# A gated attention unit and an MLP in one kernel: second batch's z moved up, blank matmuls at the start, four squares on GpSimd

## The chip, the cores and the metric

The kernel runs on one NeuronCore of a Trainium2 chip. Its engines work side by side, each through its own queue in order, and wait for each other by semaphores: TensorE (PE) does matmuls, VectorE (DVE) and ScalarE (ACT) do elementwise work, GpSimd (POOL) does elementwise work on SBUF and issues some of the DMAs, SyncE (SP) issues the others. The metric is the device time of one execution in microseconds (us); less is better.

## The reference

```python
def _attn_ref(u, v, z):                       # u, v: 8 x 3008 x 256, z: 8 x 3008 x 64
    scores = (1.0 / S) * np.matmul(z, z.transpose(0, 2, 1))
    attn = np.maximum(scores, 0.0) ** 2
    return u * np.matmul(attn, v)

def _moe_ref(x, w_in, w_out):                 # x: 24064 x 256, w_in: 256 x 2048, w_out: 2048 x 256
    h = x @ w_in
    g = h * (1.0 / (1.0 + np.exp(-1.702 * h)))
    return g @ w_out
```

The second function works on the rows that the first one makes: attention with squared relus in place of a softmax, gated by u, and then a two-layer MLP with a quick GELU.

## The kernel before

**Units.** A batch has 3008 rows. They are cut into six supercolumns of 512 rows (the last has 448), and one batch and supercolumn is a unit; there are 48. For a unit the kernel makes the scores of all 3008 rows of z against its 512 columns, in 12 pairs of two 128-row tiles. `scores` (L250) issues the two matmuls of a pair into one PSUM tile of 128x1024 (there are two such tiles, shared with the hidden layer), `relu` (L290) reads it into a 128x1024 f16 tile on ACT or DVE, and `squared` (L276) squares that tile in place, on ACT or DVE. `values` (L393) multiplies the squares with v, tile by tile ("products" below, matmuls of 64x256, always two at a time on the two halves of the array). The sums leave PSUM in two parts on ACT or DVE (`leave`, L380), POOL adds the parts (`add`, L376) and multiplies by u (`gate`, L418).

**Symmetry.** Scores are symmetric, so within a batch later units reuse squares of earlier ones: SP turns a square tile with a DMA transpose into a tile T (`turn`, L231, the issue at L242), and units from the fourth on (NDIR = 3) read these. The turned rows of units are also transposed (`turn_x`, L318) and swapped in halves (`swap_x`, L336) to feed the MLP.

**Where squares lie.** Most squares lie in a ring of 14 tiles. For units 0 and 1, pairs 6 to 11 lie in buffers that are not needed yet (`home`, L200): unit 0's in the second v buffer V16[1], unit 1's in the second turned z, ZT[1], and in z16. These must be read out before the second batch's z and v are loaded there.

**The second batch's z.** `load_z` (L105) issues three DMAs from POOL into z16, `turn_z` (L116) copies z beside itself on POOL (L118) and lets SP transpose it into ZT (L119). The first scores of unit 6 read ZT[1]. v comes in four quarters (`load_v`, L98). All of these are hooked to places in the order of work by `at` (L593): `at(n, j, ...)` runs when unit n's products reach its tile j. Each starts with `hold` (L221), a small POOL copy that reads the newest square, so that POOL's queue waits until that square is there. W1 is loaded by eight POOL DMAs at (0, 13) (L112), W2 by one at (1, 12) (L602).

**The MLP.** `hidden` (L486) makes two 128-column tiles of the hidden layer for 512 rows, ACT takes the sigmoid (L500), DVE multiplies (L504), and `outs` (L520) multiplies with w_out (L531). It runs LAG = 3 units behind the attention.

**The order of work.** The order is not written out by hand. The Python code that builds the program keeps a clock for each engine (`now`) and a price for each operation (`cost`, L131), and hands out work in the order that these give: `work` (L556) is the fixed order of products and outputs on PE; between them, `filler` (L666) puts the next score pair or hidden tile, whichever is due first; `advance` (L152) gives relus, squares and sums to the engine that would end them first, and sends DMAs on SP in order of their due time. A DMA issued by POOL, a hold and the copy in turn_z have no price in that plan. What the plan fixes is only the order on each engine; on the chip, semaphores set the times.

**The start.** z of batch 0 is loaded by SP, cast, and turned on PE through PSUM (L612 to L653), while eight blank matmuls (L625) run ahead of it.

```python
home[(0, 6 + k)] = lend(V16[1].rearrange("p n d -> p (n d)"), k)
...
at(0, 12, lambda: load_u(0))
at(0, 13, load_w1, lambda: load_u(1))
at(1, 12, lambda: pool.dma_start(W2, moe_w_out.rearrange("(fo p) c -> p fo c", p=P)))
```

Of the kernel before, what the change touches and what calls it, by code (L numbers as in the profile page):

```python
# [8 lines left out]
F32 = mybir.dt.float32  # L9
F16 = mybir.dt.float16  # L10
P = 128
# [3 lines left out]
def kernel(  # L15
# [11 lines left out]
    ALU = mybir.AluOpType  # L27

    B, S, D = u.shape
# [15 lines left out]
    LAG = 3  # L45
    RING = (LAG + 1) * TB
    H = P // 2
# [50 lines left out]
    def load_v(b, q):  # L98
        rows(b, v, q * VN, (q + 1) * VN, V16[b % 2][:, q * VN:(q + 1) * VN, :], pool)
# [5 lines left out]
    def load_z(b):  # L105
        rows(b, z, 0, NJ, z16[:, :, 0, :], pool)
# [9 lines left out]
    def turn_z(b):  # L116
        turned.add(b)
        pool.tensor_copy(z16[:, :, 1, :], z16[:, :, 0, :])  # L118
        sp.dma_start_transpose(ZT[b % 2], z16.rearrange("p n a d -> p (n a d)"))  # L119
# [9 lines left out]
    T_LAT, T_SEM, T_DMA = 0.25, 0.1, 3.5  # L129
    now = {"pe": 6.0, "act": 6.0, "dve": 7.0, "pool": 6.0, "sp": 6.0}  # L130
    cost = {  # L131
        ("act", "relu"): 1.03, ("dve", "relu"): 1.23, ("act", "sq"): 1.03, ("dve", "sq"): 0.7,
        ("act", "part"): 0.6, ("dve", "part"): 0.7, ("pool", "add"): 1.1, ("act", "sig"): 1.03, ("dve", "gt"): 1.23, ("pool", "gate"): 1.2,
        ("sp", "turn"): 1.45, ("sp", "turn_x"): 2.6, ("sp", "store"): 0.6, ("sp", "swap"): 1.2,
    }
    BOTH = ("act", "dve")
# [7 lines left out]
    def push(ready, kind, engines, fn):  # L144
        nonlocal pushed
        pushed += 1
        ops.append((ready, pushed, kind, engines, fn))
# [28 lines left out]
    def pe_at(rows_, dur):  # L176
        if mode[0] != rows_:
            now["pe"] += T_SW
            mode[0] = rows_
        now["pe"] += dur  # L180
        return now["pe"] + T_LAT
# [68 lines left out]
    def scores(k):  # L250

        nonlocal nxt
        for i in range(k):
            n, t = pairs[nxt]
            nxt += 1
            b, isup = divmod(n, NIS)
            Z = ZT[b % 2]
            assert b in turned
            p_ = take_ps()
            sc = psA.tile([P, 2, ISUP], F32, name="sc", tag="A")  # L260
            for g in range(2):
                h0 = g * DQK
                pe.matmul(  # L263
                    sc[:, g, :], Z[h0:h0 + DQK, 2 * t + g, :],
                    Z[h0:h0 + DQK, isup * NIB:(isup + 1) * NIB, :],
                    start=True, stop=True,
                )
            if (n, t) in home:
                a = home[(n, t)]
            else:  # L270
                a = pap.tile([P, 2, ISUP], F16, name="ap_", tag="ap_")
                ring.append((n, t))
            A[(n, t)] = a
            a_left[(n, t)] = 2 + turns(n, t)

            def squared(e, at, n=n, t=t, a=a, isup=isup):  # L276
                if e == "act":
                    act.activation(a, a, AF.Square, scale=1.0)
                else:
                    dve.tensor_tensor(a, a, a, ALU.mult)  # L280
                if isup == NIS - 1 and t == NP - 1:
                    pool.memset(a[:, 1, ISUP - SREM:], 0.0)
                    at += 0.5
                A_at[(n, t)] = at
                latest[0] = a
                if turns(n, t):
                    key = (n - isup + t // 2, isup)
                    send(at, "turn", NDIR if n == 1 and (n, t) in home else key[0], lambda at: turn(n, t, at), lambda: key in T or len(colors) > 0)

            def relu(e, at, p_=p_, sc=sc, a=a, squared=squared):  # L290
                if e == "act":
                    act.activation(a, sc, AF.Relu, scale=CSC)
                else:
                    dve.tensor_scalar(a, sc, 0.0, CSC, ALU.max, ALU.mult)
                set_ps(p_, at)
                push(at, "sq", BOTH, squared)

            push(pe_at(H, T_SC), "relu", BOTH, relu)

# [64 lines left out]
    def half(x, g):  # L364
        return x[g * H:(g + 1) * H]
# [227 lines left out]
    def at(n, j, *fns):  # L593
        def go():
            hold()
            for f in fns:
                f()
        side[(n, j)] = go
# [4 lines left out]
    for b in range(1, B):  # L603
        n0 = (b - 1) * NIS
        late = b == 1
        at(n0 + 1 + 2 * late, 13, lambda b=b: load_z(b))
        at(n0 + 2 + 2 * late, 13, lambda b=b: turn_z(b))
        for q in range(VQ):
            at(n0 + 3 + late + q // 2, (EDGE, 12)[q % 2], lambda b=b, q=q: load_v(b, q))


    NZ = NJ // 4  # L612
# [18 lines left out]
    def turn_q(q):  # L631
        ztps.append(psB.tile([P, NZ, P], F16, name="ztp", tag=f"B{q % 2}{q // 2}"))
        for jj in range(NZ):
            pe.transpose(ztps[q][:, jj, :], z16[:, q * NZ + jj, :, :].rearrange("p a d -> p (a d)"), ident)  # L634
# [13 lines left out]
    cast_z(3)  # L648
    keep_q(2)
    turn_q(3)  # L650
    now["pe"] = 8.0
    advance(7.0)
    keep_q(3)  # L653
# [12 lines left out]
    def filler():  # L666

        p_ = ps_free[ps_next % 2]
        if p_ is None or p_ > now["pe"]:
            return None  # L670
        can = []
        if nxt < len(pairs) and pairs[nxt][0] // NIS in turned and min(now["act"], now["dve"]) < now["pe"] + 0.8:
            old = len(ring) - NA
            if pairs[nxt] in home or old < 0 or not a_left[ring[old]]:
                can.append((urgent(("a",) + pairs[nxt], 3.0), "a"))
        if hnext < len(hids) and hnext - outs_done < NG and now["act"] < now["pe"] + 1.5 and now["dve"] < now["pe"] + 2.0:
            m = hids[hnext][0]
            xt = xt_at[m * TB // 64:(m + 1) * TB // 64]
            if None not in xt and max(xt) <= now["pe"]:
                can.append((urgent(("h",) + hids[hnext], 5.0), "h"))  # L680
        return min(can, default=None)

    wi = 0
    while wi < len(work):
        advance(now["pe"])
        w = work[wi]
        r = ready_of(w)
        late = r is None or r > now["pe"]
        f = filler()
        if f:  # L690
            if f[1] == "a":
                scores(1)
            else:
                hidden(*hids[hnext])
                hnext += 1
            continue
        if late:
            step = min([t for t in [r, ps_free[ps_next % 2]] + [o[0] for o in ops + sends] + [now[e] for e in ("act", "dve", "pool", "sp")] if t is not None and t > now["pe"]], default=now["pe"] + 0.1)
            now["pe"] = step
            assert now["pe"] < 2000.0  # L700
            continue
        if w[0] == "o":
            key = (w[1], w[2][0])
            if key in side and w[3] == 0:
                side.pop(key)()
            values(*w[1:])
        elif w[0] == "r":
            halves(w[1])
        elif w[0] == "s":
            shorts(w[1])  # L710
        else:
            outs(*w[1:])
        wi += 1
# [34 lines left out]
```

## Time and profile before

| | us |
|---|---|
| median of three runs | 1251.13 (1250.79, 1251.19, 1251.13) |
| the profiled execution | 1251.23 |
| its span, first to last instruction | 1249.3 |
| PE busy | 1228.6 (98%) |
| weight loads (PEld) busy | 1011.8 (81%) |
| DVE busy | 937.6 (75%) |
| ACT busy | 819.1 (66%) |
| POOL busy | 472.5 (38%) |

The profile is of one execution. A group's row names the line of the kernel, the engine, the operation, what it writes and reads, with shapes, how often, the busy time and the mean duration. "sc" is a score tile, "ap", "V", "ZT" and "z" as targets of L292, L294, L278 and L280 are relus and squares (the last three in borrowed buffers), "O" the sums of a unit, "hg" the hidden layer, "yps" the output. The granted clock is 1.00 when PE runs at full speed. A matmul's shown duration includes its latency; the pace of PE is better read from the chain of waits, where back-to-back products take 0.87 us for 16 and a score pair 0.22.

### The profile page before, as it was taken

How to read it: one execution, taken by the hardware profiler on the slowest of the kernel's cores; microseconds unless marked ns; L12 is line 12 of the kernel's file. 1: busy time of each engine (PE TensorE's matmuls, PEld its weight loads, DVE VectorE, ACT ScalarE, POOL GpSimd, SP SyncE). 2: the span in 40 equal slices, each digit the busy share in tenths (PEclk: the TensorE clock that was granted, in tenths of full speed). 3: DMA queues.
4: the chain of work that ended last, by engine and by line, in shares of the span. 5: the costliest groups of instructions: out<-in, count | busy, mean ns of one | idle time of the engine just before them, and what ended most of it. 6: DMA issues, size and time to landing. Idle time of an engine off the chain costs nothing.

```text
span 1249.3 us, 41891 instructions
## 1 busy us (share of the span) xinstructions
PE 1228.6 (98%) x18584; PEld 1011.8 (81%) x18584; DVE 937.6 (75%) x906; ACT 819.1 (66%) x933; POOL 472.5 (38%) x447
## 2 busy tenths in 40 slices
PE   8998999999999999999999999999999999999998
PEld 5876789988998877888778887788877888778886
DVE  7975877777888778876788768877688776877556
ACT  7855676666767657766577656676566765766444
POOL 5443334332433324343343424343343434332331
PEclk8999999999999999999999999999999999999999
DMA  9997887766986939889398684969759877574211
GB/s 151 172 166 153 145 138 131 133 132 123 133 149 135 154 91 143 142 138 165 77 142 155 128 147 90 139 125 166 131 105 141 161 127 119 112 137 110 67 45 60
DMA packets 442135, 161.74 MB, mean 129 GB/s; under 512 B 351841, under 2 KB 441953, under 8 KB 441953
## 3 DMA queue, kind: packets, MB, share of 16 engines
q1 hardware_dynamic: 390528, 141.62, 59.0%
q0 software_dynamic: 51424, 17.44, 13.8%
q8 instruction: 145, 2.38, 0.8%
q14 instruction: 38, 0.30, 0.1%
HBM read 60.29 MB, written 24.64 MB: 68 GB/s over the span
## 4 chain that ended last, share of the span: by engine, by line
PE 93%; DVE 5%; issue 1%; DMA 0%; ACT 0%; DVEq 0%; ACTq 0%
PE O L403 36%; PE hg L493 25%; PE yps L531 24%; PE sc L263 6%; PE O L478 1%; DVE GT L504 1%; PE O L465 1%; DMA ZT<-z 0%; PE warm L625 0%; DVE sums L384 0%; PE ztp L634 0%; DVE ap__8041 L280 0%; DVE ap__2880 L280 0%; DVE ap__713 L280 0%; DVE ap__18581 L280 0%
## 5 line engine op out<-in xcount | busy, mean ns | idle before, releaser
L504 DVE TENSOR_TENSOR GT<-hg,tsg 128x1024 f16<-128x1024 f32 x376 | 456.7, 1220 | 211.1 <-ACT tsg L500 209.9
L500 ACT ACTIVATE tsg<-hg 128x1024 f16<-128x1024 f32 x376 | 380.9, 1023 | 274.8 <-PE hg L493 248.2
L377 POOL TENSOR_TENSOR sums<-sums 128x512 f32<-128x512 f32 x188 | 249.0, 1325 | 666.4 <-ACT sums L382 349.4
L493 PE MATMUL hg<-XT,W 64*128 64x512 f16 x1504 | 387.9, 376 | 3.0 <-DVE GT L504 1.9
L531 PE MATMUL yps<-W,GT 64*128 64x256 f16 x6016 | 374.2, 270 | 1.3 <-DVE GT L504 0.9
L493 PE MATMUL hg<-XS,W 64*128 64x512 f16 x1504 | 370.3, 376 | 0.0
L531 PEld LDWEIGHTS <-GT 64*128 64x128 f16 x6016 | 324.1, 94 | 47.5 <-DVE GT L504 1.4
L493 PEld LDWEIGHTS <-W 64*128 64x128 f16 x3008 | 175.9, 94 | 87.5 <-issue 6.1
L403 PE MATMUL O<-V,T 64*128 64x256 f16 x3392 | 217.4, 269 | 0.1
L403 PEld LDWEIGHTS <-T 64*128 64x128 f16 x3392 | 185.9, 94 | 28.1 <-issue 0.3
L419 POOL TENSOR_TENSOR X<-sums,RU 128x512 f16<-128x512 f32 (+2 forms) x104 | 140.6, 1353 | 7.8
L263 PE MATMUL sc<-ZT 64*128 64x512 f16 x688 | 126.6, 380 | 10.7 <-DMA ZT<-z 4.5
L382 ACT ACTIVATE sums<-O 128x512 f32<-128x512 f32 x114 | 65.2, 596 | 52.8 <-PE O L403 47.1
L384 DVE TENSOR_SCALAR sums<-O 128x512 f32<-128x512 f32 x78 | 52.9, 687 | 33.9 <-PE O L403 30.1
L382 ACT ACTIVATE sums<-yps 128x512 f32<-128x512 f32 x111 | 63.8, 592 | 17.1 <-PE yps L531 15.9
L384 DVE TENSOR_SCALAR sums<-yps 128x512 f32<-128x512 f32 x73 | 50.0, 685 | 14.1 <-issue 9.9
L263 PEld LDWEIGHTS <-ZT 64*128 64x128 f16 x688 | 40.1, 95 | 17.8 <-issue 7.6
L87 POOL DMA_DIRECT2D V<-in_v_dram x32 | 28.0, 878 | 0.0
L87 POOL DMA_DIRECT2D z<-in_z_dram x7 | 10.9, 1564 | 0.4 <-PE hg L493 0.4
L478 PE MATMUL O<-V,T 128*64 128x256 f16 x160 | 10.3, 275 | 0.0
L118 POOL COPY z<-z 128x1536 f16<-128x1536 f16 x7 | 10.2, 1452 | 0.0
L478 PEld LDWEIGHTS <-T 128*64 128x64 f16 x160 | 8.1, 110 | 1.9 <-issue 1.9
(1536 smaller groups left out, 1522.2 us busy)
## 6 DMA issues: line engine op xcount, KB each, us to landing
out_dram<-sums SPq DMA_DIRECT2D x92, 256.0 KB, 4.0
RU<-in_u_dram SPq DMA_DIRECT2D x40, 512.0 KB, 4.5
V<-in_v_dram POOLq DMA_DIRECT2D x24, 384.0 KB, 7.2
XS<-XT SPq DMA_DIRECT2D x60, 128.0 KB, 4.0
RU<-in_u_dram SPq DMA_DIRECT2D x8, 384.0 KB, 3.7
z<-in_z_dram POOLq DMA_DIRECT2D x7, 368.0 KB, 9.4
V<-in_v_dram POOLq DMA_DIRECT2D x8, 320.0 KB, 9.1
XT<-X SPq DMA_TRANSPOSE x144, 2.5
```

The lines of the kernel that those rows point to most:

```text
L87: eng.dma_start(dst[:, :full - lo, :], dram[b, lo * P:full * P].rearrange("(n p) d -> p n d", p=P),)
L263: pe.matmul(sc[:, g, :], Z[h0:h0 + DQK, 2 * t + g, :], Z[h0:h0 + DQK, isup * NIB:(isup + 1) * NIB, :], start=True, stop=True,)
L377: pool.tensor_tensor(s_[:, 0, :, :], s_[:, 0, :, :], s_[:, 1, :, :], ALU.add)
L382: act.activation(s_[:, g, :, :], ps[g], AF.Copy, scale=scale)
L384: dve.tensor_scalar(s_[:, g, :, :], ps[g], scale, None, ALU.mult)
L403: pe.matmul(O[g][:, i2, :], half(sq, g), half(V[:, j, :], g), start=(j == 0 and i2 == 0), stop=(ends and j == js[-1] and (i2 == 1 or short)),)
L419: pool.tensor_tensor(X[:p, :, ib:ib + k, :].rearrange("p c n d -> p n c d"), both[:p, ib - 2 * h:ib - 2 * h + k, :].rearrange("p n (c d) - ...
L478: pe.matmul(O[c0:c0 + SREM, 1, :], squares_of(n, j, NIB - 1)[:, :SREM], V[:, j, :], start=False, stop=False, tile_position=(0, c0),)
L493: pe.matmul(hg[:, e, :], half(W1[:, fg // 2, c, fg % 2 * P:(fg % 2 + 1) * P], e), half(x[:, c // 2, p0:p0 + TB], e), start=(c == 0), stop= ...
L500: act.activation(tsg, hg, AF.Sigmoid, scale=1.702 / FSC)
L504: dve.tensor_tensor(GT, hg, tsg, ALU.mult)
L531: pe.matmul(Y[g][:, i2, :], half(GT[:, e, s * P:(s + 1) * P], g), half(W2[:, ff, :], g), start=(fg == 0 and e == 0 and i2 == 0), stop=(end ...
```

## The change

There are four edits.

1. In the plan, GpSimd gets a price for squares, and pairs 7 and 10 (t % 3 == 1) of units 0 and 1 are squared by GpSimd alone.
2. For the second batch, `load_z` is hooked to (3, 8) in place of (3, 13), and `turn_z` to (4, 6) in place of (4, 13). The first quarter of v, which was at (4, 6), goes to (4, 7).
3. Where the plan has PE wait before its first products, it now issues a blank matmul (64 rows, 256 columns, into a PSUM tile of its own); there come to be 16 of them.
4. Hidden tiles of the first 512 rows are not taken as filler before unit 3.

Nothing else is edited, but the plan is made anew: the order of PE, ACT, DVE, POOL and SP differs up to PE's matmul 3421 of 18584 and is the same from there on.

```diff
-        ("act", "relu"): 1.03, ("dve", "relu"): 1.23, ("act", "sq"): 1.03, ("dve", "sq"): 0.7,
+        ("act", "relu"): 1.03, ("dve", "relu"): 1.23, ("act", "sq"): 1.03, ("dve", "sq"): 0.7, ("pool", "sq"): 2.8,
...
-                    dve.tensor_tensor(a, a, a, ALU.mult)
+                    (dve if e == "dve" else pool).tensor_tensor(a, a, a, ALU.mult)
...
-                push(at, "sq", BOTH, squared)
+                push(at, "sq", ("pool",) if (n, t) in home and t % 3 == 1 else BOTH, squared)
...
-        at(n0 + 1 + 2 * late, 13, lambda b=b: load_z(b))
-        at(n0 + 2 + 2 * late, 13, lambda b=b: turn_z(b))
+        at(n0 + 1 + 2 * late, 8 if late else 13, lambda b=b: load_z(b))
+        at(n0 + 2 + 2 * late, EDGE if late else 13, lambda b=b: turn_z(b))
         for q in range(VQ):
-            at(n0 + 3 + late + q // 2, (EDGE, 12)[q % 2], lambda b=b, q=q: load_v(b, q))
+            at(n0 + 3 + late + q // 2, (EDGE + late, 12)[q % 2], lambda b=b, q=q: load_v(b, q))
...
+    idle = psB.tile([P, D], F32, name="idle", tag="B00")
...
-            if None not in xt and max(xt) <= now["pe"]:
+            if None not in xt and max(xt) <= now["pe"] and (m or work[wi][1] >= LAG or work[wi][0] == "y"):
...
             step = min([t for t in [r, ps_free[ps_next % 2]] + [o[0] for o in ops + sends] + [now[e] for e in ("act", "dve", "pool", "sp")] if t is not None and t > now["pe"]], default=now["pe"] + 0.1)
+            if wi == 0 and step - now["pe"] > 0.08:
+
+                pe.matmul(idle, half(blank[:, 0, :P], 0), half(blank[:, 0, :D], 0), start=True, stop=True)
+                pe_at(H, T_MM)
+                continue
```

In POOL's new queue, unit 0's pair 7 is squared first; then come the two holds of (0, 12) and (0, 13) and the eight issues of W1; then the square of unit 0's pair 10; then unit 0's sums and gates; then the square of unit 1's pair 7, the hold and issue of W2, and the square of unit 1's pair 10.

## The prediction

> **What bounds the kernel now.** I read the page's slices first, then the list of waits, then a table by stretch, then the timeline around the two places where TensorE (PE) stops. The slices:
>
> ```profile
> PE   8998999999999999999999999999999999999998
> ...
> PEclk8999999999999999999999999999999999999999
> ```
>
> PE is full nearly everywhere, at full clock; only the first slice (31 us) and the third fall short. In instruction order the two kernels become the same, on every engine, from PE matmul 3421 of 18584 on, which runs at 247.5 us. So what the change is worth arises before that. The list of waits (waiter, releaser: us in total, times, longest) and the table by stretch (PE, weight loads, DVE, ACT, POOL busy; granted clock; DMA):
>
> ```profile
> PE sc L263 <- DMA ZT<-z: 4.5, 1, 4.5
> PE hg L493 <- DVE GT L504: 1.9, 2, 1.5
> PE sc L263 <- DVE ap__809 L294: 1.7, 1, 1.7
> ...
> PE sc L263 <- DVE ap__473 L294: 1.4, 1, 1.4
> ```
>
> ```profile
> 10.60:17.30 6.70, 5.75 (x50) 4.22 (x51) 4.26 (x5) 4.67 (x5) 0.00 (x0) 0.50 1.11 150
> 17.50:24.00 6.50, 6.50 (x112) 5.87 (x110) 5.80 (x7) 5.27 (x6) 2.47 (x6) 1.00 0.68 166
> 24.00:64.00 40.00, 35.37 (x572) 31.02 (x567) 38.35 (x38) 34.21 (x39) 22.37 (x19) 1.00 1.28 170
> 102.00:106.10 4.10, 0.00 (x0) 0.00 (x0) 0.00 (x0) 0.77 (x1) 2.09 (x2) 1.00 1.07 195
> 106.20:109.50 3.30, 3.29 (x30) 2.17 (x32) 1.82 (x2) 1.54 (x2) 0.57 (x2) 0.50 0.00 0
> ```
>
> Three stages: 10.6 to 17.4 at half clock, PE the bound; 24 to 64 with DVE busy 38.35 of 40 us, so DVE is the bound and PE waits for relus; and 102 to 109.5, where PE waits for the second batch's turned z and then runs at half clock.
>
> **Blank matmuls.** From 11.55 to the first matmul on unit 0's pair 10 (24.0 us) the chain of waits has full-clock pieces of 0.87 us for 16 product matmuls and 0.22 for a score pair, half-clock pieces of 1.71 and 0.43. That stretch is 140 products and 9 score pairs in the new order: 140 x 0.0547 + 9 x 0.216 = 9.6 us at full clock from 12.0 us, where the products start in both. PE gets there at 21.6, not 24.0: 2.4 to 2.6 us sooner. The 16 blanks lie in waits for relus (0.9, 0.3 and 1.1 us) and cost at most 16 x 0.109 = 1.7 us if that cover is gone. Lower bound of the gain: 0, since the clock fell at 10.5 after a stretch in which PE was 57% busy, and blanks may not keep it. I take all of it.
>
> **Four squares by GpSimd (POOL).** Pairs 7 and 10 of units 0 and 1. POOL's queue is in order, and in the new order unit 0's pair 10 stands behind two holds and W1's eight DMA issues:
>
> ```profile
> 20.40 0.17 POOL L223 COPY scrap<-V 1x2 f16<-1x2 f16 x1 [10.82 <-DVE V L280]
> 21.41 0.17 POOL L223 COPY scrap<-V 1x2 f16<-1x2 f16 x1 [0.83 <-ACT V L278]
> 21.88 4.93 POOL L112 DMA_DIRECT2D W<-in_moe_w_in_dram  x8 [0.30 <-issue]
> ```
>
> The planner gives these issues no time; they took 4.93 us. Both holds now wait for pair 9's square, on DVE, which by the sooner PE ends at about 19.5 (before, 22.4). Then 0.1 + 2 x 0.17 + 0.3 + 4.93: the square starts at 25.2. No row shows such a square. Low end: the copy L118, 1.452 us for 1536 elements, so 0.97 for 1024. High end: L377, 1.72 us for 512 when DVE interferes, so 3.44. L377 is nearest (two inputs, an elementwise operation), at its mean of 1.325: 2.65. It ends at 27.9, and PE, in order, stands at pair 10's products from 21.6: a new wait of 6.3 us (4.5 to 7.1). Behind it in PE stands the score pair that feeds relu 16; ACT and DVE run dry near 23. Behind the square in POOL stand unit 0's sums and gate, and behind those on SP the turns of X. The wait is longer than the 4.5 us after which the clock fell to a half for 3.4 us, so PE resumes at half clock: 8 products at 0.107 and a score pair at 0.43 put relu 16 on DVE at 29.3.
>
> From there DVE is the bound, as before. By the new order it has, up to the relu that releases the last score pair before the second batch (pair 44): 13 relus x 1.22 + 16 squares x 0.68 + 4 sums parts x 0.69 = 29.6 us. To this come the delays of DVE's squares beside POOL:
>
> ```profile
> 60.81 1.59 POOL L419 TENSOR_TENSOR X<-sums,RU 128x512 f16<-128x512 f32 x1
> ...
> 61.20 1.75 DVE L280 TENSOR_TENSOR ap__1085<-ap__1085 128x1024 f16<-128x1024 f16 x1
> ```
>
> A square is 0.68 alone, 1.75 here: it ends 0.55 after POOL's operation, so it waited for that operation. Eight squares between 28 and 63 us lost 6.4 us together, to twelve POOL operations that all remain: 6.4 again. The two new POOL squares of unit 1 add, by the largest of these rows, 1.07 each: 2.1 (0 to 5.3, a whole 2.65 each). Gaps of DVE: 1.0 (0 to 2). So 29.3 + 29.6 + 6.4 + 2.1 + 1.0 = 68.4, against 64.1 where the last such wait ended before. The rest up to the first output matmul (L531) is PE's own 12.2 us in both: 80.6 against 76.3. PE has then done 1.7 us less work than before (two groups of hidden matmuls fewer, from the new condition in filler). It is behind by 6.0 us at equal work.
>
> The Trainium skill, "SBUF — State Buffer", section "Who interferes with whom", has a DVE operation with two SBUF inputs wait for the whole of a GpSimd operation that reads SBUF; the pair of rows above agrees, and by it a POOL square of 2.65 us could hold DVE for nearly that long, which speaks against this change.
>
> **z sooner.** The moved part does not bind:
>
> ```profile
> 89.51 1.45 POOL L118 COPY z<-z 128x1536 f16<-128x1536 f16 x1
> ...
> 93.36 3.72 SPq L242 DMA_TRANSPOSE T<-ap__1501  x1
> 97.19 1.43 SPq L548 DMA_DIRECT2D out_dram<-sums  x2
> 98.73 1.49 SPq L336 DMA_DIRECT2D XS<-XT  x2
> 100.45 4.27 SPq L119 DMA_TRANSPOSE ZT<-z  x1
> ```
>
> z is copied by 91.0, yet SP issues its turn at 100.45, landing at 106.2: SP is behind with its queue. In the new order SP has the same 22 turns of squares, four units of XT and XS, six loads of u and two stores ahead of it. load_z's three issues (2.7 us) pass nothing on POOL; the copy passes two holds and two v loads (1.7 us of issue), so those loads come 1.5 us later and interfere less with the slow turns at 90.9 and 93.4 (2.38 and 3.72 us against 1.25 elsewhere). The turn lands between 102.6 (both turns fast) and 106.2. But PE comes later: from 80.6 it has 160 L531 matmuls, 80 hidden, 12 scores and 188 products, 29.0 us, before the first score on ZT[1]: 109.6. So the wait of 4.5 us and the half clock after it (1.6 us) go, with 3 us to spare. This is what pays.
>
> **Sum.** Before, PE reached the same amount of work (2.0 us past its first score on ZT[1]) at 106.2 + 3.3 at half clock + 0.3 = 109.8. After: 109.6. What follows is PE's own work with the small waits of before (2.4 us up to 247 us), which I cost the same. Change -0.2 us on a profiled execution of 1251.23 (span 1249.3, 1.9 around it; the median of the three runs is 1251.13): **1251.0**. Its own range: 1249 to 1253.5.
>
> **The rivals.** About 0.2% (2.5 us) is what a measurement of this kernel can tell from no change.
>
> B, POOL's squares are short. At the copy's rate (0.97) pair 10 is squared at 26.2, 1.7 us sooner, and DVE is held little by the two others (2.1 less); with a gap of DVE fewer (0.7) PE is 4.5 us earlier at 105.1, about when ZT lands: 1246.5. For: POOL's copy row. Against: L377. It decides for faster where a square takes under 1.7 us.
>
> C, each POOL square holds DVE for its whole length. Unit 1's two squares cost DVE 2 x 2.65 and not 2.1: 3.2 us more on the binding engine, 1254.2. For: five DVE squares that each lost the rest of a POOL operation. Against: DVE is mostly at relus, which read PSUM and kept 1.21 beside POOL. It decides from 2.3 us lost per square. That page's rule is this rival.
>
> D, z is not sooner and no new wait delays PE (the POOL square is hidden): then PE stands before ZT as now, gains only the 2.6 and the 2.0 us of work put ahead, 1246.6; against it stands POOL's order.
>
> **How the numbers follow.** A 0.45, B 0.20, D 0.05, C 0.30. Same 0.45, faster 0.25, slower 0.30. The range runs from B and D, less 0.5, to C with a square of 3.44 us (0.8 at pair 10, 0.8 more held): 1246 to 1256.
>
> **What would show it.** PE waiting 4 to 7 us for a POOL square at about 22 us, POOL's L280 right after eight L112 issues; a half clock near 24 to 31 us and none at 11; no wait for ZT; DVE's squares over 1.7 us beside POOL's L280; the first L531 near 80 us. If pair 10 is squared before PE comes, or ZT is still waited for, the sum is wrong at that step.

## The result: slower by 0.1 to 0.2%

The changed kernel took 1253.70 us (median of 20 executions, 1247.53 to 1255.25) against 1249.56 us (1248.69 to 1253.47) for the kernel before in the same comparison: ratio 1.0024, 95% interval 1.0015 to 1.0033 (the means, 1252.99 and 1250.03, have this ratio; the medians lie further apart). The profiled execution of it took 1251.27 us (span 1249.4), 0.04 us from the profiled one of before (1251.23). So the forecast of 1251.0 fits the one execution that has a profile and misses the typical one, and both halves of that sentence need an explanation.

**The profile after.** The slices of the page:

```profile
PE   7999999999999999999999999999999999999998
...
PEclk8999999999999999999999999999999999999999
```

The fourth slice (94 to 125 us; the prediction counted it as the third) is 9 now, and the first is 7. The longest waits of PE from 6 us on (waiter, releaser: us in total, times, longest):

```profile
PE O L403 <- POOL V L280: 4.9, 1, 4.9
PE sc L263 <- DMA ZT<-z: 2.0, 1, 2.0
PE O L403 <- DVE sums L384: 1.4, 1, 1.4
PE sc L263 <- DVE ap__872 L294: 1.1, 1, 1.1
```

The first line is new, the wait for the square by POOL. The second is the wait that the prediction said would go: it is shorter and still there. The stretches of the table shown of before (PE, weight loads, DVE, ACT, POOL busy; granted clock; DMA share; GB/s), and then the 3.4 us from 109.3 on:

```profile
10.60:17.30 6.70, 6.47 (x99) 5.42 (x97) 6.31 (x7) 5.22 (x6) 1.17 (x1) 1.00 1.14 158
17.50:24.00 6.50, 4.39 (x72) 3.60 (x66) 4.71 (x5) 6.15 (x7) 5.05 (x10) 1.00 0.79 142
24.00:64.00 40.00, 34.98 (x530) 28.71 (x532) 33.28 (x34) 26.67 (x32) 23.91 (x18) 0.92 1.13 173
102.00:106.10 4.10, 4.10 (x70) 3.61 (x66) 3.08 (x4) 2.50 (x5) 3.24 (x3) 1.00 1.28 242
106.20:109.50 3.30, 1.34 (x22) 1.07 (x24) 0.91 (x1) 0.98 (x1) 2.02 (x2) 0.97 0.00 0
...
109.30:112.70 3.40, 3.40 (x26) 1.49 (x22) 1.11 (x2) 1.67 (x2) 0.16 (x1) 0.50 0.55 85
```

The half clock of 10.5 to 17.4 is gone, as predicted. Another one stands from 23.95 to 30.78 (the 0.92), behind the wait for POOL's square, and another from 109.28 to 112.70, behind the wait for ZT. From 24 to 64 DVE is busy 33.3 us, not 38.4.

The two places where PE stops, in the timelines of POOL and SP (start, us, engine):

```profile
19.81 4.97 POOL L112 DMA_DIRECT2D W<-in_moe_w_in_dram  x8
24.70 1.99 POOL L280 TENSOR_TENSOR V<-V 128x1024 f16<-128x1024 f16 x1
...
89.93 1.45 POOL L118 COPY z<-z 128x1536 f16<-128x1536 f16 x1
...
91.46 0.90 POOL L87 DMA_DIRECT2D V<-in_v_dram  x1
...
92.47 0.83 POOL L87 DMA_DIRECT2D V<-in_v_dram  x1
...
94.39 3.11 SPq L242 DMA_TRANSPOSE T<-ap__1554  x1
97.73 6.79 SPq L119 DMA_TRANSPOSE ZT<-z  x1
```

The square stands on POOL right behind W1's issues, as predicted; PE, whose last matmul before it starts at 21.6, goes on at 26.75. The turn of ZT is issued 2.7 us sooner than before (100.45) but occupies SP's queue 6.79 us and not 4.27, and lands at 108.11: 10.4 us after its issue, against 5.7 before. PE had come at 105.75. The two loads of v are issued at 91.46 and 92.47 (before: 87.55 and 88.56); the second lands at 103.41 (before: 97.25), so that it is under way while SP turns z.

### The profile page after: what moved, and what is told of

It is laid out like the page before. It is cut to its first block, busy times and chain, and to the rows that moved or that the text cites. A ratio compares the mean times of both kernels' runs of the same rounds, so it can differ in the third digit from the quotient of the medians.

```text
span 1249.4 us, 41917 instructions
## 1 busy us (share of the span) xinstructions
PE 1229.5 (98%) x18600; PEld 1014.5 (81%) x18600; DVE 937.4 (75%) x906; ACT 816.4 (65%) x929; POOL 480.8 (38%) x451
## 3 DMA queue, kind: packets, MB, share of 16 engines
q8 instruction: 145, 2.38, 0.8%
## 4 chain that ended last, share of the span: by engine, by line
PE 93%; DVE 4%; issue 1%; DMA 1%; POOL 1%; ACT 0%; DVEq 0%; POOLq 0%
PE O L403 35%; PE hg L493 25%; PE yps L531 25%; PE sc L263 6%; PE O L478 1%; DMA ZT<-z 1%; PE O L465 1%; DVE GT L504 0%; POOL W L112 0%; DVE sums L384 0%; PE warm L625 0%; DVE z L280 0%; DVE ZT L280 0%; DVE V L294 0%; DVE V L280 0%
## 5 line engine op out<-in xcount | busy, mean ns | idle before, releaser
L531 PE MATMUL yps<-W,GT 64*128 64x256 f16 x6016 | 375.0, 269 | 1.2 <-DVE GT L504 0.9
L531 PEld LDWEIGHTS <-GT 64*128 64x128 f16 x6016 | 325.2, 94 | 46.8 <-DVE GT L504 1.4
L263 PEld LDWEIGHTS <-ZT 64*128 64x128 f16 x688 | 40.9, 94 | 11.8 <-issue 4.2
L403 PE MATMUL O<-V,V 64*128 64x256 f16 x88 | 7.6, 312 | 4.9 <-POOL V L280 4.9
L403 PEld LDWEIGHTS <-V 64*128 64x128 f16 x88 | 5.2, 109 | 6.6 <-POOL V L280 5.1
```

The source lines that it names most:

```text
L263: pe.matmul(sc[:, g, :], Z[h0:h0 + DQK, 2 * t + g, :], Z[h0:h0 + DQK, isup * NIB:(isup + 1) * NIB, :], start=True, stop=True,)
L403: pe.matmul(O[g][:, i2, :], half(sq, g), half(V[:, j, :], g), start=(j == 0 and i2 == 0), stop=(ends and j == js[-1] and (i2 == 1 or short)),)
L531: pe.matmul(Y[g][:, i2, :], half(GT[:, e, s * P:(s + 1) * P], g), half(W2[:, ff, :], g), start=(fg == 0 and e == 0 and i2 == 0), stop=(end ...
```

## The experiments

Two explanations were tested. **L**, the late square: what costs is the square of unit 0's pair 10 on POOL behind W1's issues; z neither binds nor pays. **Z**, the collision: the loads of v beside the DMA transposes make ZT land late, and the landing sets the time. Every comparison with an interval is one of runs on the same chip, against the kernel before there.

### The changed kernel again

No edit.

> The changed kernel as it is, for a second profile and more times. Both theories: 2 to 4 us slower than the kernel before. Theory L (the late square): the profile shows TensorE waiting 4 to 6 us near 21.6 us for GpSimd's square of unit 0's pair 10, and half clock for 6.8 us after it. Theory Z (the second batch's z): the wait at the first score on ZT[1], 2.0 us in the first profile, is longer here, 4 us or more, and varies from execution to execution, which makes most executions slower than the first profile's.

1251.73 us (1248.88 to 1255.41) against 1250.13; ratio 1.0011 [1.0002, 1.0021]. In its profile (1251.36 us) the square by POOL is waited for 4.9 us, ZT 2.1, half clock from 24.07 and from 109.40, ZT issued at 97.20 and landed at 108.26. Slower again, by less, and the same picture.

### Three squares on POOL

```diff
-                push(at, "sq", ("pool",) if (n, t) in home and t % 3 == 1 else BOTH, squared)
+                push(at, "sq", ("pool",) if (n, t) in home and t % 3 == 1 and (n, t) != (0, 10) else BOTH, squared)
```

> The changed kernel, but unit 0's pair 10 is squared by ScalarE or VectorE; GpSimd keeps the other three. TensorE's order is otherwise the same. Theory L: the wait of 4.9 us and the half clock behind it (3.4 us lost) go, DVE and ACT get one square more (0.7 to 1.1 us): 5 to 7 us faster than the changed kernel up to 60 us, of which the wait for ZT[1] gives back what lies under its landing (up to 4 us): 2 to 6 us faster than the changed kernel in the end. Theory Z: the gain up to 60 us is given back whole at ZT[1], and the time stays within 1 us of the changed kernel's.

1249.33 us (1247.96 to 1250.65), ratio 0.9990 [0.9981, 0.9998]: 2.4 us less than the changed kernel beside it. The waits in its profile (1249.66 us):

```profile
PE sc L263 <- DMA ZT<-z: 5.1, 1, 5.1
PE O L403 <- DVE sums L384: 1.4, 1, 1.4
```

The wait for POOL is gone, and no half clock follows at 24. PE comes to ZT[1] at 100.11, 5.6 us sooner, but ZT lands at 105.57, and PE waits 5.1. Of 5.6 us gained, 2.4 remain in the median: the rest is given back at ZT[1]. L alone does not explain the kernel.

### No square on POOL

```diff
-                push(at, "sq", ("pool",) if (n, t) in home and t % 3 == 1 else BOTH, squared)
+                push(at, "sq", BOTH, squared)
```

> The changed kernel without its GpSimd squares: blank matmuls, z sooner and the condition on hidden tiles stay. Theory L: TensorE is 2.6 us ahead of the kernel before at the first products and loses nothing to GpSimd; it comes to ZT[1] sooner by 1 to 3 us and waits there 4.5 to 7 us for a turn that lands no sooner than 102.6: level with the kernel before to 3 us faster. Theory Z: z's turn lands later than before (108 us against 106), so 1 to 3 us slower than the kernel before.

1250.50 us (1249.39 to 1253.13), ratio 1.0003 [0.9995, 1.0012]. This is the sharpest case of Z. SP's queue in its profile (1250.01 us):

```profile
90.42 1.28 SPq L336 DMA_DIRECT2D XS<-XT  x2
91.92 9.73 SPq L119 DMA_TRANSPOSE ZT<-z  x1
```

The turn is issued 8.5 us sooner than in the kernel before and lands only 2.5 us sooner, at 103.70: 11.8 us after its issue. The loads of v were issued at 86.19 and 87.21 and the second landed at 100.44. PE waits 4.9 us.

### The changed kernel with z as before

```diff
-        at(n0 + 1 + 2 * late, 8 if late else 13, lambda b=b: load_z(b))
-        at(n0 + 2 + 2 * late, EDGE if late else 13, lambda b=b: turn_z(b))
+        at(n0 + 1 + 2 * late, 13, lambda b=b: load_z(b))
+        at(n0 + 2 + 2 * late, 13, lambda b=b: turn_z(b))
         for q in range(VQ):
-            at(n0 + 3 + late + q // 2, (EDGE + late, 12)[q % 2], lambda b=b, q=q: load_v(b, q))
+            at(n0 + 3 + late + q // 2, (EDGE, 12)[q % 2], lambda b=b, q=q: load_v(b, q))
```

> The changed kernel, but the second batch's z and v are hooked to the places of the kernel before. TensorE's order is the same as in the changed kernel. Theory L: the z part neither binds nor pays; within 1 us of the changed kernel. Theory Z: the two v loads start 3 us sooner and are done when ZT's transpose is issued, it takes 5.7 us to land and not 10.4: 2 to 4 us faster than the changed kernel.

Two groups: seven executions at 1246.78 to 1247.39 and five at 1251.09 to 1253.33; ratio 0.9992 [0.9978, 1.0006]. The median is 1247.34 us, against 1251.73 for the changed kernel on the same chip, and the means are 1249.20 and 1251.75; of the 32 executions of the changed kernel so far only one (1247.53) is as short as the first group. So in the changed kernel undoing edit 2 gains 2.5 us in the mean, as Z said. What the short executions gain was not seen: the profile (1251.33 us) is of the second group, with a wait and a landing like the changed kernel's: v issued at 89.54 and 90.56 and landed by 102.47, ZT issued at 99.52, landed at 108.22, wait 2.5. The mean granted clock, which is on record for each execution, does not part the groups: 1247.30 and 1253.33 us both have 0.996. Further profiles of it follow below.

### Blank matmuls alone

The kernel before with edit 3 only. Edit 4 is not in it, though the expectation names it; it would change nothing here: the run without squares on POOL has it, and but for one blank matmul that stands elsewhere its order on PE, ACT and DVE is the order of this run.

```diff
+    idle = psB.tile([P, D], F32, name="idle", tag="B00")
...
+            if wi == 0 and step - now["pe"] > 0.08:
+
+                pe.matmul(idle, half(blank[:, 0, :P], 0), half(blank[:, 0, :D], 0), start=True, stop=True)
+                pe_at(H, T_MM)
+                continue
```

> The kernel before with the blank matmuls alone (edits 3 and 4): the squares on ACT and DVE, z and v hooked as before. The rule that a gain is given back at ZT[1] (G): PE comes to the first score that reads ZT[1] about 2.5 us sooner (the half clock of 10.5 to 17.4 is gone), and since SP and POOL send z at the pace of their own queues, the wait for ZT grows from 4.5 to 6 to 7 us and the time stays within 0.7 us of the kernel before (1249.9). The rival (K): the landing of ZT moves forward with PE, the wait stays near 4.5 and the time is 2 to 2.6 us less, 1247.5.

1249.80 us (1248.03 to 1250.68) against 1249.81; ratio 0.9995 [0.9986, 1.0003]. In its profile (1248.45 us) the early half clock is gone, PE comes to ZT[1] at 98.70 (before: 101.33), ZT lands at 103.36 and the wait is 4.3. The wait did not grow as "given back" (G) said, and the one execution that was seen is 2.8 us shorter, but the medians are the same to 0.01 us: the median follows G, the one profile K (the landing moves with PE). Beside the run without squares on POOL, which has this order and edit 2 besides, it shows what edit 2 does: there the turn of ZT is issued 5.2 us sooner (91.92 against 97.15) and lands 0.3 us later (103.70 against 103.36).

### z sooner alone

The kernel before with edit 2 only.

```diff
-        at(n0 + 1 + 2 * late, 13, lambda b=b: load_z(b))
-        at(n0 + 2 + 2 * late, 13, lambda b=b: turn_z(b))
+        at(n0 + 1 + 2 * late, 8 if late else 13, lambda b=b: load_z(b))
+        at(n0 + 2 + 2 * late, EDGE if late else 13, lambda b=b: turn_z(b))
...
-            at(n0 + 3 + late + q // 2, (EDGE, 12)[q % 2], lambda b=b, q=q: load_v(b, q))
+            at(n0 + 3 + late + q // 2, (EDGE + late, 12)[q % 2], lambda b=b, q=q: load_v(b, q))
```

> The kernel before with edit 2 alone: load_z at (3, 8), turn_z at (4, 6), v's first quarter at (4, 7). PE's order is that of before. The prediction's step 3: SP's turn of ZT is issued by 100 and lands 6 us later, the wait of 4.5 shrinks by what the turn comes sooner. The theory of the collision (Z): the copy of z is at 90 as before, the two loads of v go out right behind it, the turn's issue is not sooner than 96 and its DMA takes 9 to 11 us beside v's quarters, so it lands at 105.5 or later; wait 3.5 to 5.5, half clock after it, time 1249 to 1251 (no change of over 0.2%). If step 3 was right but for its collision with the other edits, the wait is under 1.5 us, no half clock stands near 106, and the time is 1245 to 1246.5.

1250.30 us (1249.28 to 1254.18), ratio 1.0005 [0.9996, 1.0014]. The longest wait of its profile (1250.75 us), and SP's queue:

```profile
PE sc L263 <- DMA ZT<-z: 7.3, 1, 7.3
```

```profile
88.75 2.08 SPq L242 DMA_TRANSPOSE T<-ap__1458  x1
90.95 5.31 SPq L242 DMA_TRANSPOSE T<-ap__1501  x1
...
100.18 4.29 SPq L119 DMA_TRANSPOSE ZT<-z  x1
```

z is copied at 84.69, 4.8 us sooner, and the turn is still issued at 100.18 and lands at 106.08, as before (100.45, 106.16): SP's queue sets the issue, and the two turns of squares ahead of it are the slow ones beside v's loads (issued at 86.22 and 87.24). Edit 2 alone does nothing to the landing. That the issue is not sooner was the prediction's reading of before. This profile also has no half clock at 10.5, without any blank matmul.

### All of v later

```diff
-            at(n0 + 3 + late + q // 2, (EDGE + late, 12)[q % 2], lambda b=b, q=q: load_v(b, q))
+            at(n0 + 3 + late + q // 2 if not late else 5, (EDGE, 12)[q % 2] if not late else (6, 8, 10, 12)[q], lambda b=b, q=q: load_v(b, q))
```

> The changed kernel with all four quarters of v hooked at (5, 6), (5, 8), (5, 10) and (5, 12), so that none of v's loads is under way while SP turns z. Theory Z (the turn is slow because v's loads collide with it): the turn lands 5 to 6.5 us after its issue, at 103 to 104.5, the wait for ZT is gone, no half clock near 109, and the time falls by 2 to 4 us against the changed kernel, to 1247.5 to 1249.5, with less spread. Theory L (the square on POOL behind W1's issues is the whole cost, z neither binds nor pays): the time stays at 1251.5 to 1253.5. Under both, the wait for POOL's square (4.9) and the half clock behind it stay.

1246.94 us (1246.78 to 1247.65) against 1249.81: ratio 0.9975 [0.9965, 0.9985]. One edit, which removes no work, makes the changed kernel faster than the kernel before. SP's queue in its profile (1246.83 us), and the DMA issues between 85 and 110 us (out<-in, count, median us from issue to landing), first of this kernel, then of the changed one:

```profile
94.02 1.36 SPq L242 DMA_TRANSPOSE T<-ap__1554  x1
95.61 4.30 SPq L119 DMA_TRANSPOSE ZT<-z  x1
```

```profile
T<-ap__1554 SPq DMA_TRANSPOSE x1, 4.9
ZT<-z SPq DMA_TRANSPOSE x1, 6.2
```

```profile
T<-ap__1554 SPq DMA_TRANSPOSE x1, 9.5
ZT<-z SPq DMA_TRANSPOSE x1, 10.4
```

Without v's loads the same two turns land after 4.9 and 6.2 us in place of 9.5 and 10.4; ZT lands at 101.84 and PE, which comes at 105.26, 0.5 us sooner than in the changed kernel, does not wait, and no half clock follows there. The wait for POOL's square (4.9) is still there, with one half window behind it (25.55 to 28.96). Z is confirmed and L, as the whole cost, is refuted.

### W1 later

```diff
-    at(0, 13, load_w1, lambda: load_u(1))
+    at(0, 13, lambda: load_u(1))
+    at(1, 7, load_w1)
```

> The changed kernel with W1's eight loads hooked at (1, 7) in place of (0, 13), so that the square of unit 0's pair 10 stands on POOL behind a hold or two and not behind W1's issues. Theory L: the wait for POOL's square falls from 4.9 to under 1 us, no half clock between 24 and 31; what comes of it is then given back at ZT[1] as in the run with three squares, so 1248.5 to 1249.5. If the turn followed PE: 1246 to 1247.5. The rival that W1's issues are not what the square waits for (its own length or the hold's square is): the wait stays above 3 us and the time at 1251 to 1253.

1250.99 us (1245.23 to 1251.98), ratio 0.9998 [0.9986, 1.0009]. POOL's queue and the longest wait before 60 us in its profile (1251.09 us):

```profile
29.92 4.97 POOL L112 DMA_DIRECT2D W<-in_moe_w_in_dram  x8
34.81 1.36 POOL L419 TENSOR_TENSOR X<-sums,RU 128x512 f16<-128x512 f32 x1
36.03 1.98 POOL L280 TENSOR_TENSOR ZT<-ZT 128x1024 f16<-128x1024 f16 x1
```

```profile
PE O L403 <- POOL scrap L223: 4.8, 1, 4.8
```

Unit 0's pair 10 is squared at 19.76, but the eight issues now stand ahead of unit 1's pair 7, and PE waits for that one instead, from 32.9 to 38.1 (the list names the hold on POOL that ends with it). The place was badly chosen; it shows all the same that the wait goes where the issues go.

### Three squares on POOL and v later

The edits of the run with three squares and of the run with v later together.

```diff
-                push(at, "sq", ("pool",) if (n, t) in home and t % 3 == 1 else BOTH, squared)
+                push(at, "sq", ("pool",) if (n, t) in home and t % 3 == 1 and (n, t) != (0, 10) else BOTH, squared)
...
-            at(n0 + 3 + late + q // 2, (EDGE + late, 12)[q % 2], lambda b=b, q=q: load_v(b, q))
+            at(n0 + 3 + late + q // 2 if not late else 5, (EDGE, 12)[q % 2] if not late else (6, 8, 10, 12)[q], lambda b=b, q=q: load_v(b, q))
```

> The changed kernel with v's quarters at (5, 6) to (5, 12) and three squares on POOL (unit 0's pair 10 on ACT or DVE). In the runs so far the last matmul came 1136.7 us (squares on ACT and DVE) or 1134.5 us (squares on POOL) after ZT landed, plus half of the half clock after that, whatever went before. With the landing no longer held up by v's loads and no wait for POOL's square, PE comes to ZT[1] at 100 to 101 as in the run with three squares, ZT lands between 97 and 102: last matmul at 1235 to 1238, time 1242 to 1245. If the early gain were lost in any case (the rival: SP's queue, not v's loads, sets the landing near 102 to 104): wait 2 to 4 us, 1244.5 to 1247.

1241.65 us (1241.49 to 1247.04) against 1250.47: ratio 0.9939 [0.9924, 0.9955], 8.8 us less than the kernel before and the fastest of all by median. The clock's slices, PE's longest waits from 6 us on and the turn, in its profile (1241.66 us):

```profile
PEclk9999999999999999999999999999999999999999
```

```profile
PE O L403 <- DVE sums L384: 1.4, 1, 1.4
PE sc L263 <- DVE ap__872 L294: 1.1, 1, 1.1
```

```profile
94.55 3.65 SPq L119 DMA_TRANSPOSE ZT<-z  x1
```

ZT lands at 100.14, PE does not wait for it, and no half clock stands before the last matmul. One of the six executions took 1247.04 us; it was not seen in a profile.

### The kernel before with v later

```diff
-            at(n0 + 3 + late + q // 2, (EDGE, 12)[q % 2], lambda b=b, q=q: load_v(b, q))
+            at(n0 + 3 + late + q // 2 if not late else 5, (EDGE, 12)[q % 2] if not late else (6, 8, 10, 12)[q], lambda b=b, q=q: load_v(b, q))
```

> The kernel before with v's quarters alone moved, to (5, 6), (5, 8), (5, 10) and (5, 12). If v's loads set the landing of ZT there too: issue at 94 to 97 in place of 100.45, landing at 100 to 103 in place of 106.2, wait 0 to 2 in place of 4.5, time 1244.5 to 1247.5. If before's turn was late for SP's own queue and its waits (it lands 5.7 after issue there, v's second quarter had landed at 97.3): issue near 100, wait near 4.5, time 1249 to 1250.5.

1246.31 us (1242.34 to 1248.23), ratio 0.9967 [0.9955, 0.9980]. In its profile (1247.65 us) the turn is issued at 96.70 in place of 100.45, lands at 102.56, and is waited for 2.6 us. SP's queue is held 1.26 and 1.40 us by the two turns of squares ahead, where it was held 2.38 and 3.72. So v's loads held up the kernel before too, through the turns of squares ahead on SP rather than through ZT's own.

### v later and W1 at (2, 6)

The edit of the run with v later, and

```diff
-    at(0, 13, load_w1, lambda: load_u(1))
+    at(0, 13, lambda: load_u(1))
+    at(2, 6, load_w1)
```

> The changed kernel with v's quarters at (5, 6) to (5, 12) and W1's loads at (2, 6), where no square is left on POOL to stand behind them. All four squares on POOL. Theory L: no wait for POOL over 1 us (the run with W1 at (1, 7) only moved the wait of 4.8 to unit 1's pair 7), no half clock from 24 to 31, PE at ZT[1] at 100 to 102, time 1242 to 1245.5 as with three squares. The rival that GpSimd's squares cost by themselves (they hold DVE or come too late without W1 too): waits for POOL or DVE of 2 us or more before 50 us, PE at ZT[1] at 104 or later, 1246 to 1248.

1246.01 us (1240.07 to 1248.10), ratio 0.9960 [0.9944, 0.9975]. In POOL's timeline of its profile (1244.02 us) unit 0's pair 10 is squared before any issue of W1:

```profile
19.30 1.88 POOL L280 TENSOR_TENSOR V<-V 128x1024 f16<-128x1024 f16 x1
```

PE waits for no square of POOL; it comes to ZT[1] at 98.78, 7 us sooner than the changed kernel. All four squares on POOL cost PE little where no DMA issues stand ahead of them. But ZT lands at 102.35 here, 7.3 us after its issue, and PE waits 3.2; the kernel with three squares is faster.

### Further profiles

The changed kernel, unchanged, for an execution of another length:

> The changed kernel unchanged, for one more profile, to see an execution of another length than 1251.3. By the sum of the other runs the last matmul comes 1134.5 us after ZT lands, plus half of the half clock behind that. An execution of 1253 to 1255 should show ZT landing at 109.5 to 111.5, or a second half window after it (1.7 us each). If ZT lands at 108.2 with one half window as in the two profiles so far, the time is 1251.3 within 0.3.

1253.11 us. ZT landed at 108.88 and the half clock behind it has two windows (granted clock in the column before the DMA share):

```profile
108.90:111.10 2.20, 2.17 (x20) 1.38 (x22) 1.52 (x2) 0.26 (x1) 0.00 (x0) 0.50 0.59 118
111.20:114.50 3.30, 3.30 (x24) 1.38 (x20) 0.20 (x1) 1.29 (x2) 0.16 (x1) 0.50 0.50 159
```

The changed kernel with z as before, twice:

> The changed kernel with z as before, once more, for a profile of its shorter executions. At 1246.8 to 1247.4: no wait for ZT over 0.5 us, ZT landing at 105.4 or sooner, v's second quarter landing by 100, no half clock near 108. At 1251 to 1253: as in the profile so far, wait 2 to 3.5, ZT at 108 to 109.

> As for the other look at this kernel: shorter executions without a wait for ZT and with ZT landing at 105.4 or sooner, longer ones with a wait of 2 to 3.5 and ZT at 108 to 109.

1251.50 and 1249.82 us. Neither is of the group at 1246.8 to 1247.4, so that group stays unseen. ZT landed at 108.60 and 108.36. The second is 1.7 us shorter than the first with almost the same landing, and the clock says why: its two half windows both lie at the early wait, and none behind ZT:

```profile
25.40:32.00 6.60, 5.87 (x50) 3.81 (x52) 2.42 (x3) 1.62 (x2) 3.00 (x3) 0.50 1.45 156
106.10:108.30 2.20, 0.27 (x4) 0.00 (x0) 0.00 (x0) 1.02 (x1) 2.12 (x2) 1.00 0.12 25
108.50:112.00 3.50, 3.50 (x49) 2.26 (x49) 1.82 (x2) 1.90 (x3) 0.20 (x2) 1.00 0.38 75
```

### Three squares, v later, z as before

The kernel with three squares and v later, and

```diff
-        at(n0 + 1 + 2 * late, 8 if late else 13, lambda b=b: load_z(b))
-        at(n0 + 2 + 2 * late, EDGE if late else 13, lambda b=b: turn_z(b))
+        at(n0 + 1 + 2 * late, 13, lambda b=b: load_z(b))
+        at(n0 + 2 + 2 * late, 13, lambda b=b: turn_z(b))
```

> The kernel with three squares on POOL and v at (5, 6) to (5, 12), with z loaded at (3, 13) and turned at (4, 13) as before. If edit 2 brings the turn forward once v is out of the way: z copied some 2 us later than with edit 2 (84.3 there), the turn lands later than PE comes (100.3), a wait of 1 to 3 us and a half clock, time 1243 to 1246. If SP's own queue sets the turn and edit 2 does nothing (the theory so far): turn issued at 94.5 within 1 us, landing at 100 to 101, no wait over 0.5 us, time 1241.5 to 1242.

1243.54 us, in two groups, 1241.27 to 1241.83 and 1245.25 to 1246.07 (three each); ratio 0.9948 [0.9934, 0.9963]. The profile (1241.41 us) has z copied at 84.39 (with edit 2: 84.31), the turn issued at 94.42 and landed at 99.98, and no wait. POOL's queue holds z's copy back to the same moment under both hooks. So in the executions that were seen edit 2 neither gains nor costs once v is out of the way; whether it keeps executions out of the second group is open. That group is not one of more half clock: an execution of 1245.92 us has a mean granted clock of 1.000, like one of 1241.83.

## Why the prediction was wrong

**One sum holds for every execution with a wait for ZT.** Take the first score matmul on ZT[1], which starts when ZT lands, and the last matmul, and subtract half of the half clock between them. What is left is the same each time, whatever went before (times are starts of matmuls and of SP's issue, in us; "PE comes" is the last matmul ahead of the wait):

| profile | PE comes | ZT issued | ZT lands | half clock after | last matmul | the rest |
|---|---|---|---|---|---|---|
| before | 101.33 | 100.45 | 106.16 | 3.3 | 1244.58 | 1136.71 |
| blanks alone | 98.70 | 97.15 | 103.36 | 3.4 | 1241.80 | 1136.69 |
| z sooner alone | 98.47 | 100.18 | 106.08 | 2.7 | 1244.11 | 1136.65 |
| no square on POOL | 98.46 | 91.92 | 103.70 | 5.9 | 1243.35 | 1136.66 |
| before, v later | 99.67 | 96.70 | 102.56 | 3.4 | 1240.98 | 1136.67 |
| changed | 105.75 | 97.73 | 108.11 | 3.4 | 1244.36 | 1134.49 |
| changed, second profile | 105.79 | 97.20 | 108.26 | 3.4 | 1244.48 | 1134.47 |
| changed, third profile | 105.36 | 99.66 | 108.88 | 5.6 | 1246.19 | 1134.45 |
| z as before (1251.33) | 105.36 | 99.52 | 108.22 | 3.4 | 1244.41 | 1134.45 |
| z as before (1251.50) | 105.36 | 99.52 | 108.60 | 3.0 | 1244.59 | 1134.45 |
| z as before (1249.82) | 105.99 | 99.18 | 108.36 | 0.0 | 1242.91 | 1134.50 |
| three squares | 100.11 | 97.72 | 105.57 | 5.6 | 1242.80 | 1134.42 |
| W1 later | 103.51 | 97.57 | 107.08 | 5.8 | 1244.47 | 1134.43 |
| W1 at (2, 6), v later | 98.78 | 95.10 | 102.35 | 0.0 | 1236.87 | 1134.47 |

The rest is 1136.7 where no square is on POOL and 1134.5 where some are, because the new order puts 36 more matmuls, 2.0 us of PE's work, ahead of ZT[1]. Another 6.6 to 7.2 us lie after the last matmul's start and outside the span. So where PE waits for ZT, all that happens earlier counts only as far as it moves the landing or the clock behind it. In the three kernels with v later in which it does not wait (four squares; three squares, with z hooked either way), PE's own arrival counts.

**The step that failed** is the one on z: "So the wait of 4.5 us and the half clock after it (1.6 us) go, with 3 us to spare. This is what pays." Both numbers behind it were off, towards each other. PE came at 105.75, not 109.6; and ZT landed at 108.1 to 108.9, not between 102.6 and 106.2. The upper end of the landing was taken from before, with the argument that v's loads "come 1.5 us later and interfere less with the slow turns". They came 3.9 us later and interfered more, with ZT's own turn: later was the wrong direction. Before, POOL's timeline had them at

```profile
87.55 0.90 POOL L87 DMA_DIRECT2D V<-in_v_dram  x1
...
88.56 0.83 POOL L87 DMA_DIRECT2D V<-in_v_dram  x1
```

and after, at 91.46 and 92.47. About half of it, 1.9 us, is edit 2, which puts z's copy ahead of them; the other 2.0 us is that POOL came to this place later (with z's hooks as before they were issued at 89.54). The runs with v later show that the loads are the cause. Neither the forecast nor one of its three rivals had ZT landing later. Rival C's 1254.2 lies near the median of 1253.7, but by luck: its mechanism, a DVE held for 5.3 us by two squares that then makes PE late, did not come about (2.3 us, and PE came sooner than said).

**Why the profiled execution looked right.** In it, the later landing (+2.0 us) and the smaller rest (-2.2 us) cancel, with one half window behind ZT in both. That is a coincidence of two profiles. The third profile of the changed kernel adds 0.8 us of landing and 1.1 us for more of a second half window, and comes to 1253.11. The forecast was summed against a profiled execution of 1251.23 that is itself 1.7 us above the median of 20 executions of the kernel before. What a typical execution of before at 1249.6, or one of the changed at 1254, looks like was not seen; that they differ by the number of half windows behind ZT and by some landing would fit the sum (one half window is worth 1.7 us), but is argued, not shown. The mean granted clocks on record speak for it in part. Of the 90 executions of the kernel before that ran beside the experiments, the 35 with 0.995 took 1251.0 us in the mean and the 26 with 0.997 took 1249.5. For the changed kernel, 12 of the 20 have 0.996, from 1251.27 to 1254.83, and 0.001 of the clock is worth 1.25 us: these hold about the same amount of half clock, so what parts them is where it lies, or when ZT lands.

**Blank matmuls.** Right in the first part: no half clock from 10.5 on, the pair 10 products reached at 21.6 as said. But the gain was an item of one execution. The profile of z sooner alone has no half clock there without blanks, that of before with v later has one window and not two. And alone the blanks left the median where it was.

**The square behind W1.** Right in kind and place: PE waits for POOL's L280 behind eight issues of L112 (4.97 us; 4.93 was used), then runs at half clock. Mis-sized: a square of POOL took 1.89 to 2.01 us, not 2.65, so PE waited 4.86 us, not 6.3, and relu 16 came at 28.25, not 29.3.

**DVE's lag behind it.** Oversized, and DVE was not the bound to the end of it. The sum gave 39.1 us from relu 16 to the last score pair before the second batch; it took 36.4 (28.25 to 64.68, where 68.4 was said). PE's last wait for a relu ended at 54.24, and it came to that pair without one. Delays of DVE's squares beside POOL came to 6.1 us where 6.4 + 2.1 was said. The part of the two new squares was right, 2.3 us:

```profile
37.77 1.13 DVE L280 TENSOR_TENSOR ZT<-ZT 128x1024 f16<-128x1024 f16 x1
...
40.67 2.53 DVE L280 TENSOR_TENSOR z<-z 128x1024 f16<-128x1024 f16 x1
```

```profile
36.34 2.01 POOL L280 TENSOR_TENSOR ZT<-ZT 128x1024 f16<-128x1024 f16 x1 [0.29 <-ACT ZT L292]
...
40.73 1.91 POOL L280 TENSOR_TENSOR z<-z 128x1024 f16<-128x1024 f16 x1
```

The first two lines are of DVE's timeline, the others of POOL's, in the changed kernel. DVE's squares end 0.55 us after the POOL square that they ran beside, so they lost 0.45 and 1.85 us. That second one is rival C's case, a square of DVE held nearly the whole length of POOL's, but for one square only. The Trainium skill, "SBUF — State Buffer", section "Who interferes with whom", says that a DVE instruction with two SBUF inputs contends with GpSimd's reads for a lock; the 2.53 us agree. The other squares of DVE met fewer sums and gates than before (3.8 us lost, 6.4 before). The first L531 came at 77.02, not 80.6, and from there to ZT[1] PE needed 28.7 us, 29.0 was said. So 3.6 of the 3.9 us by which PE came sooner than said had arisen by the first L531: 1.05 at relu 16, the rest in the stretch that was summed as DVE's.

## What to carry to other kernels

Find the one transfer that PE waits for, and ask what shares the DMA engines with it and with the queue ahead of it: moving a load out of its way, with no work less, took the changed kernel from 1.0024 and 1.0011 to 0.9975 of the kernel before, and the kernel before itself to 0.9967, while engine time saved ahead of such a wait was given back there in part (three squares) or, in the median, whole (blank matmuls). Before a new operation goes on GpSimd's queue, look which DMA issues stand ahead of it there; a square behind eight issues kept PE waiting for 4.9 us, and with the issues moved to the wrong place another square did so again. And where one clock window is worth as much as the effect, see first where the profiled execution lies among many runs before a sum is made against it.

## What was not expected of the hardware

- But for the last one of each execution, the stretches of half clock last 3.41 or 6.83 us, and the same order of work shows none, one or two such windows after the same wait: behind waits of 2.0 to 3.2 us for ZT, 0.0 (z as before, 1249.82), 3.4 and 5.6 us of half clock. The wait of 4.9 us for POOL's square was followed by 6.83, 6.83 and 3.41 us in the three profiles of the changed kernel. In each of the 17 profiles the changes of the clock lie whole multiples of 3.413 us apart (the 88.75 us of full clock between the two half stretches of the kernel before are 26 of them), and this grid lies differently from execution to execution. What a wait costs hangs on how the grid cuts it: in the changed kernel the wait for ZT left PE idle for 2.04 us of one window, and the next was at half clock; in z as before (1249.82) the grid cut a wait of 2.04 us into 0.84 and 1.20, and no window was. In all profiles, a window at full clock with 2.00 us or more of idle PE was followed by one at half clock, and one with 1.87 us or less was not, but for one in the first 11 us of the kernel before (1.46). A window at half clock was followed by another where PE was idle in it for 0.85 us or more, and by full clock where for 0.75 or less. These bounds are read off afterwards; no run sets the grid. The Trainium skill, "TensorE: Matmul & The Clock Gate", Part 1, says that the activity window is 3413 ns long and free-running; the grid agrees.
- In the 17 profiles the DMA transpose of ZT landed 5.6 to 7.9 us after its issue where v's loads had landed or not begun, and 8.7 to 11.8 us after it with one of them under way. The Trainium skill, "DMA: Bandwidth & Descriptors", section "SWDGE vs HWDGE vs iDMA", has loads issued by GpSimd and those issued by SP feed different queues of the same 16 engines, which take turns between them; the slower turns agree.
- GpSimd squared 128x1024 f16 in place in 1.88 to 2.34 us, where DVE takes 0.68 alone.
